# A fused retention and soft mixture-of-attention kernel: gates and scaling factors moved to the head of a step, logits copied with v, scaling split from transposing, three buffers of p, a new tail

## The chip, the cores and the metric

One core of one Trainium2 chip runs the whole program. The time is device microseconds of that core for one execution; lower is better. The engines are TensorE (PE, with weight loads PEld), VectorE (DVE), ScalarE (ACT), GpSimd (POOL), and SyncE (SP), whose queue issues every DMA. TensorE writes its results to PSUM, which has eight banks; a bank can be written again only when its readers are done.

## The reference

Inputs q, k, v have the shape [8, 8, 576, 64] (batch, heads, positions, width). Everything is float32.

```
ret  = (0.125 * q @ k.T) * gamma_h ** (i - j)   for i >= j, else 0
x    = (ret @ v), heads side by side            # [8, 576, 512]
g    = x @ w_gate                               # logits of 4 experts
w    = softmax over the two largest of g, 0 for the others
out  = sum over experts e of  w_e * softmax(causal(0.125 * (x wq_e)(x wk_e).T)) @ (x wv_e) @ wo_e
```

Each expert has a width of 64, so that two experts fill 128 partitions.

## The kernel before

**Chunks and steps.** A batch has five chunks of positions, t = 0 to 4: four of 128 and one of 64. The 40 chunks of the eight batches are numbered n = 5b + t. The main loop runs over steps n = 0 to 41; a step works on several chunks at once, each at another stage, so that all engines have something to do.

**What a step does, in the order in which it is written.** `load(n + 2)` brings q, k (tile x) and v, k (tile vk) of a later chunk. `qk(n)` makes the products of q and k of chunk n in blocks of 64 (L137), ScalarE copies them to p (L140), GpSimd masks them (L143). `result(n - 1)`, a generator called `late`, makes the retention output of the chunk before: products with the running state (`old`, L165, copied by ScalarE in L168), products with the masked p (`own`, L178), their sum on VectorE (L183), the scaling by gamma on GpSimd (L188), the split in two parts for a two-part multiplication (ScalarE L191, GpSimd L193), and on the way `decay` of a later chunk's v (GpSimd, L104). `state(n)` updates the running state (L117, VectorE L123 and L125). `scores(n - 6)` makes the attention scores of an older chunk m into PSUM (`ss`, L338, or L345 for t = 4), VectorE subtracts the row maximum on the way out of PSUM (L356, L360), ScalarE takes the exponential and its row sum (L364). `work(n)` holds the large matmuls: projections to q and k (`proj`, L235), the value projection (`vproj`, L260), the product of attention weights and values (`values`, L400) and the output projection (`outproj`, L420, copied out by ScalarE in L423). Its five steps are, by n mod 5: 3, projections of q and k for a batch's first two chunks; 0, value tiles of these (and half an output projection); 1, projections for the other three chunks; 2, value tiles of these, with `values` of the batch before woven in; 4, output projections.

**Gates and the scaling of p.** `vproj` makes the four logits beside the values in one PSUM bank; ScalarE copies the values to vn (L264), then VectorE copies the logits to lg (L265). After a group's last tile `gate` goes on a list. Each call of `gates()` advances every gate on the list by one phase: first seven VectorE operations (L292 to L301) and an exponential on ScalarE (L302), then nine small VectorE operations that end in the weights WT (L304 to L311). `spread(m)` of a chunk m first makes the factors, gate weight over row sum, in three small VectorE operations (L376 to L378). Then it goes through up to four blocks: scale the block of p32 (ScalarE, L385; for two blocks of t = 3 VectorE, L383) and transpose it in 32x32 pieces into TA or TB (VectorE, L387 and L389). `values` reads TA and TB. `spread` is a generator: `work` yields between groups of matmuls, and each yield lets it do one block. In a step with `values` the flag `hold` keeps all of `spread` until `work` is done, since the transposes overwrite what `values` still reads.

**Order.** PE, DVE, ACT and POOL execute their instructions in the order in which the Python code issues them (`manual_schedule`). SP's queue is ordered by the program's scheduler. PSUM tiles all come from one pool of eight banks.

**The end.** The last four chunks' scores and the last batch's products run in `tail(m)`, called for m = 36 to 40.

## Time and profile before

| | |
|---|---|
| median of three runs | 482.8 us (478.55, 484.5, 482.8) |
| the profiled execution | 481.82 us |
| its span in the trace | 478.3 us |
| busy: PE, PEld | 425.9 us (89%), 369.6 us (77%) |
| busy: DVE, ACT, POOL | 307.7 us (64%), 278.4 us (58%), 172.4 us (36%) |
| mean granted TensorE clock | 0.943 of full speed |
| moved by DMA | 66.73 MB, 140 GB/s over the span |

Busy times are unions of instructions; matmuls are pipelined, and PE counts as busy while one is under way, even where the next one is late. Time outside the span (481.82 less 478.3) is start and end of the program.

### The profile page before, as it was taken

What the parts mean: (1) busy time and instruction counts of PE and PEld (TensorE: products, weight loads), DVE (VectorE), ACT (ScalarE), POOL (GpSimd) and SP (SyncE); (2) the same over time, 40 slices, a digit from 0 to 9 for tenths busy, and PEclk for the clock granted to TensorE, in tenths of its full rate; (3) what the DMA queues carried; (4) which work ended last, traced back from release to release, by engine and by line L of the source; (5) the groups of instructions that cost most, each with busy time, mean ns of one, the idle gap of its engine ahead of it and who ended that gap; (6) DMA issues with size and microseconds to landing.
All of it is one profiled execution on the core that took longest, in us unless ns stands there. A gap on an engine that the chain in (4) does not pass through costs nothing. (4 is left out here: it accounts for less than half of the span.)

```text
span 478.3 us, 21378 instructions
## 1 busy us (share of the span) xinstructions
PE 425.9 (89%) x9068; PEld 369.6 (77%) x9068; DVE 307.7 (64%) x1219; ACT 278.4 (58%) x858; POOL 172.4 (36%) x198
## 2 busy tenths in 40 slices
PE   6687995998989988998989988998989989999566
PEld 3587984787879877987878877987879876986456
DVE  2743777954777476964776477963778477826750
ACT  1545666553866377653866377663766367726732
POOL 2428544541434334641444333551544432100000
PEclk9679997999989999999999999999989999899769
DMA  7926466332745264553544263641844041405211
GB/s 281 403 96 225 154 155 214 88 117 73 207 160 140 94 188 138 189 153 96 184 161 140 92 190 135 213 131 54 229 160 138 4 103 47 123 1 124 78 46 56
DMA packets 49246, 66.73 MB, mean 140 GB/s; under 512 B 4096, under 2 KB 38400, under 8 KB 49152
## 3 DMA queue, kind: packets, MB, share of 16 engines
q1 hardware_dynamic: 49152, 65.38, 43.0%
q8 instruction: 71, 1.16, 1.0%
q14 instruction: 23, 0.19, 0.1%
HBM read 50.68 MB, written 14.68 MB: 137 GB/s over the span
## 5 line engine op out<-in xcount | busy, mean ns | idle before, releaser
L364 ACT ACTIVATE p<-p,nm 128x64 f32<-128x64 f32 (+5 forms) x144 | 79.5, 553 | 76.9 <-DVE nm L356 56.2
L143 POOL TENSOR_SCALAR_AFFINE_SELECT p<-p 64x512 f32<-64x512 f32 (+1 forms) x80 | 48.8, 610 | 166.8 <-ACT p L140 164.2
L385 ACT ACTIVATE p<-p,sm 128x128 f32<-128x128 f32 (+7 forms) x128 | 63.4, 539 | 23.1 <-DVE sm L378 23.1
L387 DVE STREAM_TRANSPOSE ta<-p 128x256 f32<-128x256 f32 (+2 forms) x144 | 56.0, 394 | 28.9 <-ACT p L385 26.2
L183 DVE TENSOR_TENSOR x<-x,own 128x256 f32<-128x256 f32 (+1 forms) x80 | 26.4, 363 | 46.2 <-ACT x L168 40.2
L356 DVE CUSTOM_DVE_ANT_0 p<-ss,mask 128x128 f32<-128x128 f32 (+7 forms) x128 | 50.7, 452 | 4.0 <-PE ss L338 3.7
L188 POOL TENSOR_TENSOR x<-x,gi 128x512 f32<-128x512 f32 (+1 forms) x38 | 44.5, 1171 | 13.3 <-DVE x L183 10.0
L338 PE MATMUL ss<-k,q 64*64 64x64 f32 (+7 forms) x512 | 41.0, 408 | 4.5 <-ACT p L140 4.5
L178 PE MATMUL own<-p,vk 64*64 64x64 f32 x1152 | 31.8, 226 | 13.1 <-issue 5.6
L193 POOL TENSOR_TENSOR x1l<-x,x1h 128x512 fp32r<-128x512 f32 (+1 forms) x24 | 26.5, 1103 | 45.6 <-ACT x1h L191 45.6
L400 PE MATMUL ys<-ta,vq 32*64 32x288 f32 (+7 forms) x1152 | 35.4, 375 | 6.5 <-DVE ta L387 4.4
L178 PEld LDWEIGHTS own<-p,vk 64*64 64x64 f32 x1152 | 26.3, 137 | 15.7 <-issue 14.9
L264 ACT ACTIVATE vn<-pv 128x256 f32<-128x256 f32 x40 | 14.8, 371 | 39.5 <-PE pv L260 39.5
L400 PEld LDWEIGHTS ys<-ta,vq 32*64 32x64 f32 x1152 | 25.9, 149 | 12.8 <-issue 4.6
L117 PE MATMUL st<-vk 64*64 64x64 f32 x1024 | 27.0, 233 | 8.8 <-DVE vk L104 3.3
L265 DVE COPY lg<-pv 128x4 f32<-128x4 f32 x40 | 5.9, 149 | 43.9 <-ACT vn L264 43.4
L420 PE MATMUL po<-yh,who 128*128 128x320 f32 (+1 forms) x128 | 29.6, 312 | 3.5 <-ACT yh L408 3.5
L104 POOL TENSOR_TENSOR vk<-vk,con 128x512 f32<-128x512 f32 (+1 forms) x34 | 32.5, 956 | 0.1
L117 PEld LDWEIGHTS st<-vk 64*64 64x64 f32 x1024 | 23.1, 145 | 10.8 <-issue 4.2
L140 ACT ACTIVATE p<-qk 128x256 f32<-128x256 f32 (+1 forms) x80 | 24.3, 359 | 8.3 <-PE qk L137 8.3
L420 PEld LDWEIGHTS po<-yh,who 128*128 128x128 f32 x128 | 20.9, 194 | 10.4 <-issue 4.9
L423 ACT ACTIVATE ot<-po 128x256 f32<-128x256 f32 (+1 forms) x64 | 24.7, 403 | 7.1 <-PE po L420 5.7
(106 smaller groups left out, 1039.1 us busy)
## 6 DMA issues: line engine op xcount, KB each, us to landing
x<-xf SPq DMA_DIRECT2D x32, 512.0 KB, 4.4
vk<-vkf SPq DMA_DIRECT2D x32, 512.0 KB, 5.8
vq<-hv SPq DMA_DIRECT2D x32, 192.0 KB, 4.3
out<-ot SPq DMA_DIRECT2D x32, 160.0 KB, 2.2
vq<-hv SPq DMA_DIRECT2D x32, 128.0 KB, 3.4
out<-ot SPq DMA_DIRECT2D x32, 128.0 KB, 1.7
hv<-vn SPq DMA_DIRECT2D x8, 384.0 KB, 2.7
ta<-wraw SPq DMA_DIRECT2D x4, 512.0 KB, 8.2
```

Of the source, the lines that this page charges most:

```text
L104: (gp if n > 5 else v).tensor_mul(vv, vv, gam[:, 2 * c:2 * c + k].unsqueeze(3).to_broadcast([128, k, 4, D]))
L117: mm(ps[r][HALF[g], s, u], vk[HALF[r], s, 1, h], vk[HALF[r], s, 0, h], start=True, stop=True)
L143: gp.affine_select(w, w, pattern=[[0, 4 * k], [1, 64]], base=0, channel_multiplier=-1, compare_op=OP.is_ge, fill=0.0)
L178: mm(own[r][HALF[u], g, i], vk[HALF[r], s, 0, 2 * g + u], p[HALF[r], g, s, u], start=True, stop=True)
L188: e.tensor_mul(x32, x32, gi[:, :, t0:t0 + C])
L338: mm(ps[u][HALF[p]], q[p][HALF[z], l0 + 64 * i:l0 + 64 * i + 64], k[p][HALF[z], :ws[u]], start=True, stop=True)
L356: v.tensor_tensor_reduce(x, ps[u], mask[:, 512 - ws[u]:], -1.0, BIG, OP.add, OP.min, nm[:, u:u + 1])
L364: act(x, x, AF.Exp, bias=bias, scale=-1.0, accum_out=sm[:, 0, u:u + 1])
L385: act(x, x, AF.Copy, scale=rs[:, u:u + 1])
L387: v.transpose(TA[:, :min(nb, 8), z, k], x[:, :min(nb, 8)])
L400: mm(py[g][HALF[z], sj - s0:], vq[QUAD[g], jj, D * z:D * z + D], tt[QUAD[g]], start=(j == 0), stop=(j == 2 * s1 - 1))
L420: mm(ps, ww[:, p, d * 128:(d + 1) * 128], yy[:, p], start=(i == 0), stop=(i == 5))
```

## The change

`gates()` and the factors of the chunk that will be scaled in this step are called at the head of a step, ahead of `qk`, `result`, `state` and `scores`; a second call of `gates()` stands behind `scores`. A gate now has three phases: VectorE, the exponential alone, VectorE. ScalarE copies all 260 columns of the value bank; VectorE's copy of the logits is gone. `spread` is split in `factors`, `scale` and `turn`; in a step with `values`, `scale` runs beside `work` and only `turn` waits. p32 has three buffers in place of two, x and vk three in place of four. The projections of batch 1's first group, all in step 8 before, are shared by steps 8 and 9. The tail is one function with an order written out by hand.

```diff
-        X[n] = x = ld.tile([128, 2, 4, C], F32, name="x", tag="x", bufs=4)
+        X[n] = x = ld.tile([128, 2, 4, C], F32, name="x", tag="x", bufs=3)
-        VK[n] = vk = ld.tile([128, C // 64, 2, 4, D], F32, name="vk", tag="vk", bufs=4)
+        VK[n] = vk = ld.tile([128, C // 64, 2, 4, D], F32, name="vk", tag="vk", bufs=3)
...
-            VN[b, r] = (sb.tile([128, nt, E * D], F32, name=f"vn{r}", bufs=1),
-                        sb.tile([128, nt, E], F32, name="lg", tag="lg"),
+            VN[b, r] = (sb.tile([128, nt, NWV], F32, name=f"vn{r}", bufs=1),
                         sb.tile([128, 4 * nt, 2 * D], F32, name=f"vq{r}", bufs=2 - r))
-        vn, lg, vq = VN[b, r]
+        vn, vq = VN[b, r]
...
-        act(vn[:, ti], ps[:, :E * D], AF.Copy)
-        v.tensor_copy(lg[:, ti], ps[:, E * D:])
+        act(vn[:, ti], ps, AF.Copy)
...
-            nc.sync.dma_start(hv.rearrange("(t p) c -> p t c", p=128), vn)
+            nc.sync.dma_start(hv.rearrange("(t p) c -> p t c", p=128), vn[:, :, :E * D])
...
-        lg = VN[b, r][1]
+        lg = VN[b, r][0][:, :, E * D:]
...
+        yield False
         act(ex, ex, AF.Exp)
         yield False
...
-        p32 = sb.tile([128, n, w], F32, name="p32", tag="p32", bufs=2)
+        p32 = sb.tile([128, n, w], F32, name="p32", tag="p32", bufs=3)
...
-    def spread(m):
+    def factors(m):
         b, t = divmod(m, 5)
         r = 0 if t < 2 else 1
         ti = t - RNG[r][2][0]
-        p32, sm, ws = SS.pop(m)
+        p32, sm, ws = SS[m]
         n = len(ws)
         rs = sm[:, 1, :n]
         v.tensor_scalar(sm[:, 0, :n], sm[:, 0, :n], 1e-9, None, op0=OP.add)
         v.reciprocal(rs, sm[:, 0, :n])
         v.tensor_mul(rs, rs, WT[b, r][:, ti].rearrange("p i z -> p (i z)")[:, :n])
-        for u in range(n):
-            z, k, nb = u % 2, 2 * t + u // 2, ws[u] // 32
-            x = p32[:, u, :ws[u]]
-            if t == 3 and u < 2:
-                v.tensor_scalar(x, x, rs[:, u:u + 1], None, op0=OP.mult)
+
+    def scale(m):
+        p32, sm, ws = SS[m]
+        for u, w in enumerate(ws):
+            x = p32[:, u, :w]
+            if m % 5 == 3 and u < 2:
+                v.tensor_scalar(x, x, sm[:, 1, u:u + 1], None, op0=OP.mult)
             else:
-                act(x, x, AF.Copy, scale=rs[:, u:u + 1])
-            x = x.rearrange("p (j c) -> p j c", c=32)
+                act(x, x, AF.Copy, scale=sm[:, 1, u:u + 1])
+            yield
+
+    def turn(m):
+        p32, sm, ws = SS.pop(m)
+        for u, w in enumerate(ws):
+            z, k, nb = u % 2, 2 * (m % 5) + u // 2, w // 32
+            x = p32[:, u, :w].rearrange("p (j c) -> p j c", c=32)
             v.transpose(TA[:, :min(nb, 8), z, k], x[:, :min(nb, 8)])
             if nb > 8:
                 v.transpose(TB[:, :nb - 8, z, k - 4], x[:, 8:])
             yield
 
+    def spread(m):
+        a, b = scale(m), turn(m)
+        for _ in a:
+            next(b)
+            yield
+
...
-            if b or kind[-1] == "1" or kind in ("o0", "y"):
+            if n == 8:
+                STEPS[8], STEPS[9] = [(b, kind, 0)], [(b, kind, 1)]
+            elif b or kind[-1] == "1" or kind in ("o0", "y"):
                 STEPS.setdefault(n, []).append((b, kind, part))
...
-    def tail(m):
+    def tail():
         b = B - 1
-        if m < NC:
-            run(scores(m))
+        t0 = NC - 5
+
+        def beside(g, *hs):
+            for _ in g:
+                for h in hs:
+                    next(h, None)
+
+        def outs(b, r):
+            for d in range(4):
+                yield from outproj(b, r, d)
+
         gates()
-        hold = m == NC - 4
-        spreads = spread(m - 1)
-        for n in {NC - 4: (NC + 2,), NC - 3: (NC + 4,), NC - 2: (NC + 5,)}.get(m, ()):
-            for _ in work(n):
-                if not hold:
-                    next(spreads, None)
-        if m == NC - 1:
-            run(values(b, 0, 4))
-            for d in range(4):
-                run(outproj(b, 0, d))
-        run(spreads)
-        if m == NC:
-            run(values(b, 4, 9))
-            for d in range(4):
-                run(outproj(b, 1, d))
+        factors(t0)
+        run(scores(t0 + 1))
+        sc = scale(t0)
+        ys = values(b - 1, 0, 9)
+        for t in RNG[1][2]:
+            beside(vproj(b, 1, t), sc)
+            next(ys, None)
+            if t == 3:
+                run(scores(t0 + 2))
+        factors(t0 + 1)
+        gates()
+        run(scale(t0 + 1))
+        gates()
+        run(turn(t0))
+        run(turn(t0 + 1))
+        gates()
+        factors(t0 + 2)
+        run(scores(t0 + 3))
+        beside(outs(b - 1, 0), spread(t0 + 2))
+        run(scores(t0 + 4))
+        factors(t0 + 3)
+        beside(outs(b - 1, 1), spread(t0 + 3))
+        run(values(b, 0, 4))
+        factors(t0 + 4)
+        beside(outs(b, 0), spread(t0 + 4))
+        run(values(b, 4, 9))
+        run(outs(b, 1))
 
...
         late = result(n - 1) if 1 <= n <= NC else iter(())
+        gates()
+        if n > LAG:
+            factors(n - LAG - 1)
...
         if n >= LAG:
             run(scores(n - LAG))
+        gates()
         if n > 5:
             run(late)
         else:
             decay(n + 1)
-        gates()
         for w in {2: "kq", 3: "v", 6: "o"}.get(n, ""):
             weights(w, "l" if w == "k" else "hl")
-        spreads = spread(n - LAG - 1) if n > LAG else iter(())
-        hold = any(kind == "y" for _, kind, _ in STEPS.get(n, []))
+        spreads, turns = iter(()), iter(())
+        if n > LAG:
+            if any(kind == "y" for _, kind, _ in STEPS.get(n, [])):
+                spreads, turns = scale(n - LAG - 1), turn(n - LAG - 1)
+            else:
+                spreads = spread(n - LAG - 1)
         for _ in work(n):
-            if not hold:
-                next(spreads, None)
+            next(spreads, None)
         run(spreads)
+        run(turns)
         run(late)
-    for m in range(NC - 4, NC + 1):
-        tail(m)
+    tail()
 
 
 def _layout(inputs):
```

## Rows read from the trace of the kernel before

**Rows 1.** Windows: start:end, length, busy us (instructions) by engine, granted clock, DMA

```profile
250.00:300.00 50.00, 45.84 (x1079) 40.20 (x1081) 32.59 (x135) 30.41 (x98) 19.98 (x23) 0.97 0.44 139
82.20:85.70 3.50, 3.50 (x21) 2.56 (x22) 2.73 (x13) 0.63 (x4) 3.04 (x4) 0.51 0.01 2
461.10:468.00 6.90, 4.46 (x128) 4.17 (x136) 2.43 (x9) 1.44 (x2) 0.00 (x0) 0.51 0.01 2
```

**Rows 2.** Waits, all of the span: who waited for whom, us in total, times, longest

```profile
ACT p L385 <- DVE sm L378: 23.1, 24, 1.8
...
PE own L178 <- ACT ot L423: 3.2, 6, 0.7
...
PE own L178 <- DVE lg L265: 1.8, 2, 1.0
```

**Rows 3.** Timeline, 274 to 285 us, after values: start, length, instruction [idle before <-releaser]

```profile
275.44 1.55 DVE L409 TENSOR_TENSOR yl<-ys,yh 128x288 fp32r<-128x288 f32 x4 [1.05 <-ACT yh L408]
...
277.50 1.17 ACT L385 ACTIVATE p<-p,sm 128x64 f32<-128x64 f32 x4 [1.19 <-DVE sm L378]
277.88 1.14 DVE L387 STREAM_TRANSPOSE ta<-p 128x64 f32<-128x64 f32 x4 [0.41 <-ACT p L385]
...
278.99 1.68 PE L338 MATMUL ss<-k,q 64*64 64x320 f32 x16 [1.27 <-ACT p L140]
...
279.84 0.75 DVE L183 TENSOR_TENSOR x<-x,own 128x256 f32<-128x256 f32 x2 [0.82 <-ACT x L168]
...
280.61 0.74 PE L235 MATMUL pj<-xh,whk 128*128 128x256 f32 x4
...
283.08 0.20 DVE L292 TENSOR_TENSOR gd<-lg 128x48 f32<-128x48 f32 x1
...
284.54 0.16 DVE L378 TENSOR_TENSOR sm<-sm,wt 128x4 f32<-128x4 f32 x1
```

**Rows 4.** Timeline, 286 to 295 us: chunk of t = 3 beside output projections

```profile
288.43 0.75 DVE L183 TENSOR_TENSOR x<-x,own 128x256 f32<-128x256 f32 x2 [1.28 <-ACT x L168]
...
291.41 0.27 DVE L304 SCALAR_TENSOR_TENSOR ex<-rk,ex 128x12 f32<-128x12 f32 x1
...
293.25 1.28 POOL L193 TENSOR_TENSOR x1l<-x,x1h 128x512 fp32r<-128x512 f32 x1 [1.60 <-ACT x1h L191]
...
293.44 1.11 DVE L378 TENSOR_TENSOR sm<-sm,wt 128x4 f32<-128x4 f32 x1
...
294.58 0.56 ACT L385 ACTIVATE p<-p,sm 128x320 f32<-128x320 f32 x1 [1.15 <-DVE sm L378]
```

**Rows 5.** Groups by form, VectorE: busy us, mean ns of one, idle before

```profile
L301 DVE TENSOR_TENSOR ex<-lg,mx 128x8 f32<-128x8 f32 x8 | 7.5, 940 | 0.3
```

**Rows 6.** Timeline, 79 to 85 us: step 9 into step 10

```profile
79.83 2.02 ACT L385 ACTIVATE p<-p,sm 128x320 f32<-128x320 f32 x4 [1.39 <-DVE sm L378]
...
82.17 2.46 PE L345 MATMUL ss<-k,q 64*64 64x288 f32 x16 [4.52 <-ACT p L140]
```

**Rows 7.** Timeline of the tail, 432 to 465 us

```profile
432.74 1.41 PE L338 MATMUL ss<-k,q 64*64 64x320 f32 x16
...
433.24 1.55 DVE L409 TENSOR_TENSOR yl<-ys,yh 128x288 fp32r<-128x288 f32 x4 [1.05 <-ACT yh L408]
...
443.44 0.62 DVE L356 CUSTOM_DVE_ANT_0 p<-ss,mask 128x448 f32<-128x448 f32 x1
...
445.76 0.17 DVE L304 SCALAR_TENSOR_TENSOR ex<-rk,ex 128x12 f32<-128x12 f32 x1
...
447.27 0.17 DVE L376 TENSOR_SCALAR sm<-sm 128x4 f32<-128x4 f32 x1
...
460.18 0.45 DVE L387 STREAM_TRANSPOSE ta<-p 128x256 f32<-128x256 f32 x1 [2.17 <-ACT p L385]
...
463.54 4.72 PE L400 MATMUL ys<-ta,vq 32*64 32x160 f32 x124 [4.42 <-DVE ta L387]
```

**Rows 8.** The page, DMA issues: KB each, median us from issue to landing

```profile
vk<-vkf SPq DMA_DIRECT2D x32, 512.0 KB, 5.8
```

More of the change, by code (lines that the diff above doesn't have):

```diff
@@ L395, in values @@
             sj = max(s0, j // 2)
-            vq, jj = VN[b, 0 if j < 8 else 1][2], j % 8 if j < 8 else j - 8
+            vq, jj = VN[b, 0 if j < 8 else 1][1], j % 8 if j < 8 else j - 8
             for z in range(2):
```

## The prediction

> **What bounds the kernel now.** I read the windows first, for the middle of the run and for stretches at a low clock, then the list of waits, then the timeline of the places where that list puts the waits of TensorE. In the middle, PE is busy 45.84 of 50 us at a granted clock of 0.97, while DVE has 32.59 and ACT 30.41 [rows 1]. So there are about 4 us in 50 that PE does not fill, and an edit on another engine can win only out of these, out of stretches at half clock, and out of the two ends. The waits that name the lines of the change are: ACT's scaling behind the factors, 23.1 us in 24 places; PE's own product behind the copy of the logits, 1.8 us in two, and behind ACT's copies of output projections, 3.2 us in six [rows 2]. The large one is a wait of ACT, which is not the bound; what it is worth has to be read in the places where PE waits for ACT afterwards. There are two such places in each batch, and then the ramp and the tail.
>
> **After values (the step with n mod 5 = 3), six times in the main loop.** Before, VectorE finishes yl at 276.99, then makes the factors, ACT scales four blocks (1.17 us), VectorE transposes them, and only behind the scalings does ACT copy the new qk banks; the scores wait 1.27 us for that bank and start at 278.99 [rows 3]. The change takes scaling away from here: it runs beside the value tiles, on an ACT that waits there anyway. The scores could then start some 1.3 us earlier. But the next projection (280.61) starts only when the scores are through and VectorE's L183, at 279.84, has freed own's bank, and L183 has a new line in front of it: four transposes (1.14 us) and, at the head of the step, the first phase of the gate with the factors, which here took from 283.08 to 284.70, 1.62 us [rows 3]. 276.99 + 1.14 + 1.62 = 279.75 against 279.84. With the overlap of adjoining VectorE operations I take 0.15 us a batch, **0.9 us** in all. The ends are 0 (L183 is no earlier) and 1.27 x 6 = 7.6 us (the projection gets another bank); the value lies near the first, because the line in front of L183 adds up to what stood there.
>
> **The chunk of t = 3 beside output projections (n mod 5 = 4), six times.** Here VectorE does the row maxima, then the last gate phase and the factors, from 291.41 to 294.55, 3.14 us; ACT meanwhile stands 1.15 us before its first scaling at 294.58, and behind the scalings come the copies of six output banks for which PE waits in the next step [rows 2, 4]. One of these factor operations, L378, took 1.11 us against 0.16 us elsewhere, exactly while GpSimd ran L193 from 293.25 for 1.28 us [rows 3, 4]; L301 in its narrower form has a mean of 940 ns over eight [rows 5]. Moved to the head of the step these operations have no such neighbour in this timeline, so the line is 3.14 - 0.95 = 2.19 us. VectorE sat idle 1.28 us before L183 there [rows 4]; the rest, 0.91 us, delays L183, the maxima and the exponentials. ACT, free at 293.43 before (294.58 - 1.15), is then free at 294.34 and need not wait: 0.24 us earlier than 294.58. Six times that is **1.5 us**. The ends: the whole wait of 1.15 us, 6.9 us in all, and a loss of 0.91 us each, 5.5 us, if PE has to wait for the bank that L183 frees. I take the sum along the line, since both its halves come from this very step.
>
> The Trainium skill, in SBUF — State Buffer, section Who interferes with whom, says that a VectorE instruction with two inputs from SBUF contends with a GpSimd instruction that reads SBUF, and that the one issued first blocks the other for its whole length. The trace agrees for L378 beside L193. The same rule speaks against the new place if GpSimd's masking of p falls beside it; by it the moved line would keep its 3.14 us, ACT would be free 1.86 us later at 295.29, and these steps would lose 0.7 us each, 4.3 in all, instead of winning 1.5.
>
> **Logits copied with v.** A value bank is now free when ACT has copied it, not when VectorE comes to L265 behind its transposes. The two waits of PE on that copy go: **1.8 us** [rows 2]; the ends are 0, where another reader of the bank is as late, and 1.8, as no other wait of that list's kind is on PE's own product. Four more columns for ACT on 256 are under 2% of a copy that PE is not waiting for. The DMA to HBM still takes rows of 256 values.
>
> **The ramp.** Step 9 had no projections; ACT waited 1.39 us for the factors, and PE stood idle 4.52 us before the scores at 82.17 [rows 6], then ran at a granted clock of 0.51 until 85.7 [rows 1]. Two projections now fill part of that gap. ACT's chain, which ends the gap, gains the same 0.24 us as above. Whether the clock stays up is not shown; that is worth half of 3.5 us, 1.75. I take both, **2.0 us**, since more than half of the gap is filled; the ends are 0.5 us lost (the projections' copies stand in ACT's queue) and 4.5 us, all of the gap.
>
> **Buffers.** A third p32 lets a scaled but not yet transposed chunk wait; without it the next exponentials would have to. For x and vk one buffer less means that a load starts when `own` of the chunk before is through, one step nearer to its use. A vk load lands 5.8 us after its issue [rows 8], and a step is 8.6 us from one L183 to the next (279.84 to 288.43) [rows 3, 4], with the first use behind L183 of the following step. So SP's queue holds the load at its head, and nothing behind it is wanted before it goes. Nothing, with 1 us lost in the filling as the other end; if that cover goes, it is 5.8 us less what remains of the step.
>
> **The tail.** Chunk 37's scores (1.41 us) go ahead of the last value tile, so yl ends at about 434.79 + 1.41 = 436.2 [rows 7]. Then VectorE does, in the new order: factors and first phase (1.62) [rows 3], transposes of chunk 35 (1.14) [rows 3] and of chunk 36 (estimate 1.7, from the same row and three times the columns at a part-fixed cost), the last phase (445.76 to 447.27, 1.5 us) [rows 7], factors (0.5). That is 6.5 us, so chunk 38's maxima start at 442.7 against 443.44. From there to the last values it took 20.1 us (463.54) [rows 7]; this held the last gate phase, 1.5 us, now ahead, and 2.17 us in which VectorE waited at 460.18 for scalings that stood behind four output copies, where copies and scalings now alternate [rows 7]. Of these 3.7 us I give back 1.1, the wait for the copy yh that stays (1.05 there) [rows 7]. 0.75 + 2.6 = 3.3 us. The last values ran at a clock of 0.51 with PE busy 4.46 us [rows 1]; a wait shorter than 4.42 us may leave part of that at full speed, up to 2.2 us, of which I take 0.7. Together **4.0 us**. The ends are 6.7 us (3.7 + 0.75 + 2.2) and 2.2 us lost, if the wait for chunk 38's maxima makes another such stretch.
>
> That wait exists: PE has made four output projections by about 440 and needs a bank for chunk 39's scores, which the maxima from 442.7 on set free. The Trainium skill, in TensorE: Matmul & The Clock Gate, Part 1, says that the throttled state is the default and activity releases it; by that the tail would win 1.1 us instead of 4.0. The trace agrees that half clock follows an idle PE, at 82.2 [rows 1, 6].
>
> **Sum.** 0.9 + 1.5 + 1.8 + 2.0 + 4.0 = 10.2 us. The profiled execution took 481.8 us, 1.0 under the median of 482.8; 481.8 - 10.2 = **471.6 us**, 2.3% under the median. About 2%, that is below 473.1 or above 492.5, can be told from no change here.
>
> **The rivals.** *Only a moved wait, 0.24.* VectorE's line at the head takes all that ACT gains; both places in the batch and the ramp give nothing, and 1.8 + 4.0 stay: 476.0 us. For it: L183 comes out at the same time above. Against it: L378 loses its neighbour.
>
> *More than the line, 0.15.* ACT's whole wait of 1.15 us goes in the t = 3 steps (6.9), and the tail has its upper end (6.7): with 0.9, 1.8 and 2.0 that is 18.3 us, 463.5 us. For it: idle VectorE at other heads. Against: the 0.91 us that L183 is late.
>
> *The tail gives nothing of weight, 0.05.* Another half-clock stretch of the size seen, 2.2 us, and none of the 0.7: 4.0 - 2.9 = 1.1 us, so 474.5 us.
>
> *Slower, 0.06.* PE waits for the banks that VectorE frees late, in the t = 3 step and in one more with a gate phase, 0.91 us each, and falls to half clock once a batch, 1.75 us: 3.6 us six times, 21.4 us, less 1.8 + 2.0 + 4.0: 495 us. It decides from 3.1 us a batch on. Against it: PE is at the long projections when these banks are wanted.
>
> That the change does not do what it says could hold for the split of scaling alone: if ACT reached those scalings only after the value tiles, the first place would stay as it is. It changes the sum by 0.9 and has no chance of its own.
>
> **Chances.** The forecast has 0.50, with a range of its own from 467 to 476; about seven tenths of it lie under 473.1. With the case above it and a small part of the others, faster gets 0.54, within 2% 0.40, slower 0.06. The range from 462 to 480 takes in the moved wait, the tail's case and the larger gain, and leaves out the slower case and the outer ends.
>
> **What would show it.** After values, scores that follow the state products at once and a projection that starts with L183's end: right; a projection at the scores' end: I gave too little. In the t = 3 step, L378 at 0.16 us and a scaling without a wait on the factors; if PE's waits on output copies stay, only the 0.24 us came. In the ramp, a clock that stays up in step 10. In the tail, the last values at about 460. A PE that waits on L183 or on the maxima in the middle of the run, or loads that land after their use, would prove the sum wrong.

## The result, and the profile after

The changed kernel takes 467.12 us (median of four runs, 465.14 to 467.85) beside 483.65 us for the kernel before (four runs, 478.55 to 485.94): a ratio of 0.9686, 95% interval 0.9601 to 0.9771, faster. The forecast was 471.6 us, its range 462 to 480. The profiled execution took 466.81 us, its span is 464.9 us, its mean granted clock 0.960 (before 481.82, 478.3 and 0.943). Of the 15.0 us between the two, 13.4 lie in the span; outside it stood 3.5 us before and 1.9 after, and since later runs of the kernel before have 1.7 to 3.0 us there, I don't ascribe the 1.6 to the change. Of all the runs reported here one, of a later kernel at 470.96 us, counts as slow and is left out of that kernel's median.

I cut both spans at the first qk product (L137) of a step:

| stretch | before | after | gain | forecast |
|---|---|---|---|---|
| start to step 8 | 61.09 | 59.99 | 1.1 | 0 |
| step 8 to 12 (ramp) | 38.12 | 35.15 | 3.0 | 2.0 |
| step 12 to 39 | 295.43 | 289.64 | 5.8 | 0.9 + 1.5 + 1.8 = 4.2 |
| step 39 to the end | 83.69 | 80.14 | 3.6 | 4.0 |

In the kernels run below step 8 starts from 2.3 us earlier to 0.9 us later than before, up to 2.7 us apart with the same first steps; whether the first line is an effect stays open. In the middle a step with n mod 5 = 3 went from 11.57 to 10.91 us (five of six), one with 4 from 7.78 to 7.88; where no half-clock stretch falls into it, one with 0 went from 10.34 to 10.03, and the one with 1 behind it from 10.02 to 9.75 (n = 26: from 11.02, with a wait of 1.04 us on the copy of the logits, to 9.75). From 75 us on, stretches at half clock (granted 0.50, 1.2 of 2.4 GHz) add up to 37.7 us before and 23.9 after; at 1.2 of 2.4 GHz each costs at most half its length, so up to 6.9 of the 13.4 us came that way, through whichever step.

The windows of the changed kernel, with the columns of [rows 1]: the middle, a stretch of the tail, and the last values.

```profile
242.70:292.70 50.00, 46.35 (x1088) 40.25 (x1087) 30.09 (x134) 30.08 (x98) 20.30 (x24) 1.00 0.47 142
...
445.80:452.60 6.80, 6.71 (x48) 6.11 (x56) 3.35 (x13) 3.23 (x9) 0.00 (x0) 0.50 0.32 113
...
451.90:458.00 6.10, 5.56 (x291) 5.06 (x290) 0.66 (x3) 1.28 (x5) 0.00 (x0) 0.94 0.15 48
```

PE fills half a us more of 50 than in [rows 1], VectorE works 2.5 us less, and the last values run at 0.94, not 0.51; the half clock has moved ahead of them, to the projections behind a wait of 2 us. Its waits:

```profile
ACT p L386 <- DVE sm L377: 1.3, 1, 1.3
...
PE pj L235 <- DVE x L183: 2.8, 4, 1.0
...
PE own L178 <- ACT ot L436: 2.8, 6, 0.5
```

ScalarE's 23.1 us behind the factors [rows 2] are gone. The wait on output copies stays (3.2 before), the one on the copy of logits is not listed any more, and TensorE now waits for L183 before the projection, which it did not before (only the weight loads did, 3.6 us in six places; now 6.7). The timeline shows it, after values and in the step with t = 3:

```profile
320.84 1.55 DVE L422 TENSOR_TENSOR yl<-ys,yh 128x288 fp32r<-128x288 f32 x4 [9.34 <-ACT yh L421]
...
322.31 0.75 DVE L394 STREAM_TRANSPOSE ta<-p 128x64 f32<-128x64 f32 x4
...
322.98 0.17 DVE L290 TENSOR_TENSOR gd<-vn 128x48 f32<-128x48 f32 x1
...
323.52 1.34 PE L337 MATMUL ss<-k,q 64*64 64x320 f32 x13
...
324.78 0.16 DVE L377 TENSOR_TENSOR sm<-sm,wt 128x4 f32<-128x4 f32 x1
324.89 0.75 DVE L183 TENSOR_TENSOR x<-x,own 128x256 f32<-128x256 f32 x2
325.36 0.73 PE L235 MATMUL pj<-xh,whk 128*128 128x256 f32 x4 [0.50 <-DVE x L183]
...
334.20 0.17 DVE L377 TENSOR_TENSOR sm<-sm,wt 128x4 f32<-128x4 f32 x1
334.31 0.75 DVE L183 TENSOR_TENSOR x<-x,own 128x256 f32<-128x256 f32 x2
...
339.15 0.55 ACT L386 ACTIVATE p<-p,sm 128x320 f32<-128x320 f32 x1
```

From the start of yl to the first projection it is 4.52 us; in [rows 3] 280.61 - 275.44 = 5.17. The scores follow the state products without a wait, and the projection starts 0.47 us into L183, which stands behind gate phase and factors (322.98 to 324.94). In the step with t = 3 the last factor takes 0.17 us where it took 1.11 [rows 4], and the scaling waits for nothing. The ramp and the last values:

```profile
72.06 0.16 DVE L377 TENSOR_TENSOR sm<-sm,wt 128x4 f32<-128x4 f32 x1
...
76.75 1.00 ACT L386 ACTIVATE p<-p,sm 128x320 f32<-128x320 f32 x2
...
79.88 1.54 PE L344 MATMUL ss<-k,q 64*64 64x288 f32 x15
...
451.91 2.79 PE L413 MATMUL ys<-ta,vq 32*64 32x160 f32 x128
454.48 2.55 PE L413 MATMUL ys<-tb,vq 32*64 32x160 f32 x160
```

In the ramp the factors are made at 72 us and ScalarE scales at 76.75, where it began at 79.83 [rows 6]. The last values start 451.91 - 384.78 = 67.1 us behind step 39, before 463.54 - 394.64 = 68.9 [rows 7].

### The profile page after: what moved, and what is told of

It is laid out like the page before. It is cut to its first block, busy times and chain, and to the rows that moved or that the text cites. A ratio compares the mean times of both kernels' runs of the same rounds, so it can differ in the third digit from the quotient of the medians.

```text
span 464.9 us, 21312 instructions
## 1 busy us (share of the span) xinstructions
PE 422.9 (91%) x9068; PEld 365.9 (79%) x9068; DVE 279.8 (60%) x1179; ACT 275.7 (59%) x858; POOL 173.5 (37%) x198
## 5 line engine op out<-in xcount | busy, mean ns | idle before, releaser
L394 DVE STREAM_TRANSPOSE ta<-p 128x256 f32<-128x256 f32 (+2 forms) x144 | 53.4, 388 | 59.0 <-ACT p L386 56.5
L422 DVE TENSOR_TENSOR yl<-ys,yh 128x288 fp32r<-128x288 f32 (+2 forms) x36 | 12.7, 414 | 63.9 <-ACT yh L421 63.9
L337 PE MATMUL ss<-k,q 64*64 64x512 f32 (+7 forms) x512 | 41.8, 409 | 3.0 <-issue 1.1
L178 PE MATMUL own<-p,vk 64*64 64x64 f32 x1152 | 30.5, 222 | 8.4 <-issue 4.6
L183 DVE TENSOR_TENSOR x<-x,own 128x256 f32<-128x256 f32 (+1 forms) x80 | 26.2, 361 | 19.6 <-ACT x L168 19.6
L263 ACT ACTIVATE vn<-pv 128x260 f32<-128x260 f32 x40 | 14.9, 374 | 29.0 <-PE pv L259 28.9
L413 PE MATMUL ys<-ta,vq 32*64 32x288 f32 (+8 forms) x1152 | 31.3, 349 | 0.2 <-DVE nm L359 0.2
L436 ACT ACTIVATE ot<-po 128x256 f32<-128x256 f32 (+1 forms) x64 | 24.5, 400 | 8.7 <-PE po L433 5.5
L433 PE MATMUL po<-yl,who 128*128 128x320 f32 (+1 forms) x128 | 29.2, 310 | 0.0
```

The costliest lines, as they stand in the source:

```text
L178: mm(own[r][HALF[u], g, i], vk[HALF[r], s, 0, 2 * g + u], p[HALF[r], g, s, u], start=True, stop=True)
L337: mm(ps[u][HALF[p]], q[p][HALF[z], l0 + 64 * i:l0 + 64 * i + 64], k[p][HALF[z], :ws[u]], start=True, stop=True)
L394: v.transpose(TA[:, :min(nb, 8), z, k], x[:, :min(nb, 8)])
L413: mm(py[g][HALF[z], sj - s0:], vq[QUAD[g], jj, D * z:D * z + D], tt[QUAD[g]], start=(j == 0), stop=(j == 2 * s1 - 1))
L433: mm(ps, ww[:, p, d * 128:(d + 1) * 128], yy[:, p], start=(i == 0), stop=(i == 5))
```

## The experiments

**My theory** after this reading: the middle is won after values, where ScalarE's scalings no longer wait for factors behind yl; the ramp and the tail are won apart from it. **The rivals**: the new places at the head carry it; the split carries it; or what looks like a gain is only where half-clock stretches fell. "Step 3" below is a step with n mod 5 = 3; L183, yl and the projection are as above. Times are medians of four runs (VectorE copies logits: three), ratios to the kernel before on the same chip (480.0 to 480.8 us) with their interval. The changed kernel was not run again beside them (its kernel before had 483.65 us), so a difference of some 3 us between one of these times and its 467.1 shows nothing by itself; step lengths can be compared.

| kernel | us | ratio | step 3 (n = 23, 28) | yl to projection |
|---|---|---|---|---|
| before | 480.0 to 480.8 | | 11.57, 11.57 | 5.17 |
| factors alone | 475.49 | 0.989 (0.984 to 0.995) | 10.25, 10.26 | 3.87 |
| tail alone | 474.45 | 0.987 (0.980 to 0.994) | 11.57, 11.57 | |
| both | 470.04 | 0.978 (0.971 to 0.984) | 10.24, 10.25 | |
| changed, old tail | 470.61 | 0.978 (0.973 to 0.984) | 10.91, 10.91 | |
| changed, old places | 467.53 | 0.973 (0.967 to 0.978) | 9.80, 9.92 | 3.53 |
| changed, scaling kept back | 464.21 | 0.965 (0.959 to 0.970) | 10.74, 10.73 | 4.34 |
| changed, sum first | 475.31 | 0.987 (0.980 to 0.994) | 9.79, 10.18 | |
| changed, VectorE copies logits | 466.35 | 0.970 (0.963 to 0.978) | 10.91, 10.92 | |
| changed, step 8 undivided | 465.43 | 0.967 (0.961 to 0.973) | 10.91, 10.90 | |
| new places in the ramp only | 465.13 | 0.967 (0.964 to 0.970) | 9.80, 9.79 | |

The table has n = 23 and 28, where the gain is largest. In n = 13, 18 and 38 most of these kernels have a wait of TensorE without a releaser, or scores held up in their course, and gain less: with the factors alone these steps take 10.82, 10.97 and 11.24 us (11.56 or 11.57 before); n = 33 waits for VectorE there, before too. The last section says what these waits are.

**The factors alone**, in the kernel before: in the steps with values, ahead of the value tiles.

```diff
+        if hold:
+            factors(n - LAG - 1)
-        spreads = spread(n - LAG - 1) if n > LAG else iter(())
+        spreads = spread(n - LAG - 1, hold) if n > LAG else iter(())
```

> The kernel before with one edit: in the steps with values (n mod 5 = 2) the three factor operations of VectorE are issued ahead of the value tiles and not behind yl; nothing else moves (scaling and transposes stay behind the values). Theory: before, ScalarE's four scalings waited for these three operations, which stood behind yl in VectorE's line, and its copies of the next qk and old banks stood behind the scalings; so this alone shortens the next step (n mod 5 = 3) from 11.57 to between 10.25 and 10.9 us, as in the runs with old places and with kept-back scaling: six times 0.7 to 1.3 us, 4 to 8 us less than before on the same chip, 473 to 477 us beside 480 to 481. Rival (the three buffers of p32 did it in the run with the new tail): that step stays at 11.5 us and the time at 480 us.

```profile
272.55 1.55 DVE L417 TENSOR_TENSOR yl<-ys,yh 128x288 fp32r<-128x288 f32 x4 [1.05 <-ACT yh L416]
...
273.29 1.18 ACT L393 ACTIVATE p<-p,sm 128x64 f32<-128x64 f32 x4
...
274.80 1.69 PE L338 MATMUL ss<-k,q 64*64 64x320 f32 x16
...
276.42 0.73 PE L235 MATMUL pj<-xh,whk 128*128 128x256 f32 x4
```

This is the timeline after values. The scalings start 0.74 us behind yl's start, before 277.50 - 275.44 = 2.06 [rows 3]; scores and projection come as much earlier, 1.3 us. Three small operations moved, 5.2 us won (4.0 of them in the profile up to step 39): the theory stands, and the split is not needed for it. The 1.3 us are those of n = 23 and 28; in n = 13, 18 and 38 it is 0.7, 0.6 and 0.3 us.

**The tail alone**, in the kernel before, and **both**:

```diff
-        X[n] = x = ld.tile([128, 2, 4, C], F32, name="x", tag="x", bufs=4)
+        X[n] = x = ld.tile([128, 2, 4, C], F32, name="x", tag="x", bufs=3)
...
-        p32 = sb.tile([128, n, w], F32, name="p32", tag="p32", bufs=2)
+        p32 = sb.tile([128, n, w], F32, name="p32", tag="p32", bufs=3)
...
-    for m in range(NC - 4, NC + 1):
-        tail(m)
+    tail()
```

> The kernel before with the new tail and its buffers (three of p32, x and vk) again, but the factors of the main loop behind yl, as in the kernel before. Theory (the factors ahead of the value tiles gave the middle its part in the run with the new tail): the steps with n mod 5 = 3 take 11.5 us, step 39 starts as before within 0.6 us save for half-clock stretches, and only the end is shorter, by 2 to 3.5 us: 477 to 478.5 us beside a before of 480 to 481. Rival (the buffers gave the middle its part): 10.2 to 11 us in these steps and 470 us in all.

> The kernel before with the new tail alone, and the buffers that it needs (three of p32, three of x and vk); gates, factors, scaling, logits and steps 8 and 9 as before. Theory (the tail and the buffers are independent of the rest): up to step 39 as before within 0.5 us, so three buffers of x and vk cost nothing, and from step 39 to the end of the span 80 to 81 us in place of 83.7: 3 us less than before, 477 to 478 us beside a before of 480 to 481 on the same chip. Rival (the tail's gain hangs on the new gate phases or on the logits): 480 us or more. Rival (fewer buffers of x and vk cost something in the filling that the other parts covered): steps 3 to 12 come 1 us or more later than before.

In the run called "both" I had put the factors of the main loop ahead of `work`, which its expectation doesn't say; so it missed by 7 us, and this led to the two single runs. With the tail alone step 3 stays at 11.57 us in all six, and step 39 starts 0.1 us later than before: the buffers cost nothing and give nothing. All of its 5.5 us of span lie behind step 39, more than expected; there its stretches at half clock add up to 13.7 us, in the kernel before to 20.6, so up to 3.5 of the 5.5 us can be the clock's doing.

**The old tail** in the changed kernel (one more call of `gates()` at m = 37):

```diff
-    tail()
+    for m in range(NC - 4, NC + 1):
+        tail(m)
```

> The changed kernel with the old tail (one more call of the gates in it, since a gate has three phases now). Theory: up to step 39 nothing differs from the changed kernel (its qk product starts near 384.8 us), and from there to the end of the span it takes about 3.5 us more again, as in the kernel before (83.7 against 80.1 us): span about 468.5, time 470 to 471 us. Rival (the tail's saving was a half-clock stretch that fell otherwise): 467 to 468 us.

The time came as expected, 470.61 us, span 468.6, but not from where I expected it. Step 39 starts at 387.82, 3.0 us later than in the changed kernel, whose code is the same up to there (2.0 of the 3.0 before step 8), and from step 39 to the end it is 80.8 us, only 0.6 more. So this hit is luck, and the run does not show what the tail is worth. The wait of [rows 7] for the last transposes is back in the list of waits:

```profile
PE ys L413 <- DVE ta L394: 4.5, 1, 4.5
```

**The old places** in the changed kernel:

```diff
-        gates()
-        if n > LAG:
-            factors(n - LAG - 1)
...
+        gates()
         for w in {2: "kq", 3: "v", 6: "o"}.get(n, ""):
...
         if n > LAG:
+            factors(n - LAG - 1)
```

> The changed kernel with the gate phases and the factors at their old places (one call behind scores and late, two phases, factors ahead of work); the split of scaling and transposing, the buffers, the step 8/9 split and the new tail stay. Theory (VectorE's line bounds the step after values, and the split of scaling shortened it): without the 1.6 us of gate phase and factors in front, L183 comes right behind the transposes, the projection is then bound by the end of the scores, and the step with n mod 5 = 3 keeps its shorter length or loses another 0.3 us: 10.6 to 10.95 us against 10.93 after and 11.57 before. In the steps with n mod 5 = 4 ScalarE waits for the factors again (about 1 us each). Time 465 to 469 us. Rival (the new places carry the gain): that step goes back to about 11.5 us and the time to 470.5 to 472 us.

The first theory held for the time, and by more than the 0.3 us expected in two of the six steps (9.80 and 9.92 us); the four others take 10.46 to 11.27. Timeline after values, and in the ramp:

```profile
270.64 1.55 DVE L421 TENSOR_TENSOR yl<-ys,yh 128x288 fp32r<-128x288 f32 x4 [6.22 <-ACT yh L420]
...
272.78 0.75 DVE L183 TENSOR_TENSOR x<-x,own 128x256 f32<-128x256 f32 x2
...
274.17 0.74 PE L235 MATMUL pj<-xh,whk 128*128 128x256 f32 x4
...
79.40 1.01 ACT L385 ACTIVATE p<-p,sm 128x320 f32<-128x320 f32 x2 [2.16 <-DVE sm L376]
...
82.92 2.13 PE L343 MATMUL ss<-k,q 64*64 64x288 f32 x14
```

L183 starts 2.14 us behind yl's start, in the changed kernel 4.05: gate phase and factors at the head cost the projection 1.0 us here. In the steps with t = 3, ScalarE waits for the factors again (24.5 us in 21 places of the span) and yet these steps take 7.82 us, not more than the 7.88 of the changed kernel. What the head is good for is the ramp: with the old places the scores start at 82.92, though step 9 has the two projections; step 8 to 12 takes 37.4 us against 35.2. So the two effects cancel, 467.5 against 467.1 us.

**Scaling kept back** (`turns = spread(...)` in steps with values, nothing beside the value tiles):

```diff
-                spreads, turns = scale(n - LAG - 1), turn(n - LAG - 1)
+                turns = spread(n - LAG - 1)
```

> The changed kernel with scaling kept behind the value tiles again, together with the transposes, in the steps with values; the factors stay at the head of the step. Theory: ScalarE's four scalings stand ahead of its copies of the qk banks again, the scores start 0.4 to 0.8 us later, their end and not L183 bounds the projection, and the step with n mod 5 = 3 takes 11.1 to 11.35 us against 10.93 after and 11.57 before; the rest of the old length was the factors ahead of the scalings. Six times 0.2 to 0.4: time 468 to 470 us. Rival (the split is the whole of that place): 11.5 us or more, time 471 us. Rival (scaling is hidden either way): 10.9 us and 467 us.

```profile
267.45 1.55 DVE L422 TENSOR_TENSOR yl<-ys,yh 128x288 fp32r<-128x288 f32 x4 [9.57 <-ACT yh L421]
...
271.33 0.74 DVE L183 TENSOR_TENSOR x<-x,own 128x256 f32<-128x256 f32 x2
271.79 0.38 PE L235 MATMUL pj<-xh,whk 128*128 128x256 f32 x1 [0.41 <-DVE x L183]
```

The last expectation came nearest, and the step is even 0.18 us shorter than with the split, since L183, behind the head, sets the projection in both and comes 3.88 us behind yl's start rather than 4.05. Beside the head the split is worth nothing. Up to step 39 the run is 1.7 us ahead of the changed kernel. The other 3.6 us of its profile lie in the tail, whose code is the same, with 6.8 us at half clock in place of 13.7: that much of a single run can be the clock's doing.

**The sum first**: head behind L183 in the steps with n mod 5 = 3.

```diff
+        first = n % 5 != 3 or n <= LAG
+        if first:
+            head()
...
             next(late, None)
+            if not first:
+                head()
```

> The changed kernel with the head's gate phase and factors put behind the sum L183 in the steps with n mod 5 = 3, ahead of the state; all else stays. Theory (VectorE's line in front of L183 is what the projection waits for now): L183 starts 1.6 us earlier there, the projection starts with the end of the scores, about 0.35 to 0.5 us earlier, the waits of the projections on L183 go; the maxima and exponentials are no later. Six times that is 2 to 3 us: 464 to 465 us. Rival (another reader of the bank, or ScalarE's later start, takes its place): no change, 467 us. Rival on the other side: VectorE's state sums, now behind the gate phase, come late for the next value tiles or the scores: 468 us.

It wins its step and loses more in the next (9.67 and 9.60 us for n = 24 and 29, where the changed kernel has 7.88; 8.12 and 8.49 for n = 14 and 19): the time is 8 us longer than the changed kernel's. The timeline, in the step that starts at 272.10 and in the next:

```profile
276.39 0.74 PE L235 MATMUL pj<-xh,whk 128*128 128x256 f32 x4
...
279.09 0.48 DVE L355 CUSTOM_DVE_ANT_0 p<-ss,mask 128x320 f32<-128x320 f32 x1
...
283.75 0.33 PE L178 MATMUL own<-p,vk 64*64 64x64 f32 x4 [0.55 <-ACT k L240]
...
284.82 0.62 PE L178 MATMUL own<-p,vk 64*64 64x64 f32 x26 [0.73 <-ACT q L242]
```

The maxima start 7.0 us behind the first qk product; in the changed kernel 6.0 (326.35 - 320.34). The exponentials, and ScalarE's copies of the projections behind them, are late by as much, and PE waits for the banks. A third course, that I had priced at 1 us.

**VectorE copies the logits** again, and **step 8 undivided**, each in the changed kernel:

```diff
-        act(vn[:, ti], ps, AF.Copy)
+        act(vn[:, ti, :E * D], ps[:, :E * D], AF.Copy)
+        v.tensor_copy(vn[:, ti, E * D:], ps[:, E * D:])
```

> The changed kernel with the logits copied by VectorE again (256 columns by ScalarE, four by VectorE, into the same tile). Theory: this copy stands in VectorE's line behind transposes and holds a value bank; the gain of the change in the steps with n mod 5 = 0 (10.34 us before, 10.03 to 10.05 after, where no half-clock stretch falls into them) is its removal, since that step's length stayed at 10.02 when the gates went back to their old places: so 10.3 us again, 1.8 us in six, time 468.5 to 469 us. Rival (the bank is wanted later than either copy): 10.05 us, time 467 us, and the 0.3 us come from elsewhere.

```diff
-            if n == 8:
-                STEPS[8], STEPS[9] = [(b, kind, 0)], [(b, kind, 1)]
-            elif b or kind[-1] == "1" or kind in ("o0", "y"):
+            if b or kind[-1] == "1" or kind in ("o0", "y"):
```

> The changed kernel with both of batch 1's first projections in step 8 again. Theory: TensorE's gap ahead of step 10's scores comes back; the stretch from the qk product of step 8 to that of step 12 takes about 2 to 3 us more than after (35.2 us after, 38.1 before), half of it a longer stretch at half clock; time 469 to 470 us. Rival (the gap is bound by ScalarE's chain and not by work for TensorE): 35.2 us and 467 us.

With the copy on VectorE the steps with n mod 5 = 0 keep their length (10.04 us for n = 25): there the rival held. But in step 26, where the kernel before waited 1.04 us for this copy, a wait on it is in the list, under the tile that it writes here:

```profile
PE own L178 <- DVE vn L264: 0.5, 1, 0.5
```

That step takes 10.18 us, in the changed kernel 9.75, so the copy is worth 0.4 us in one place. For step 8 the rival held. With step 8 undivided the stretch from 8 to 12 takes 35.3 us, and the time is no longer than that of the changed kernel. Here the scores start at 79.83, 19.1 us behind step 8, in the changed kernel 19.9:

```profile
77.50 2.01 ACT L386 ACTIVATE p<-p,sm 128x320 f32<-128x320 f32 x4
79.42 0.63 ACT L140 ACTIVATE p<-qk 128x256 f32<-128x256 f32 x2
79.83 2.46 PE L344 MATMUL ss<-k,q 64*64 64x288 f32 x16 [2.62 <-ACT p L140]
```

**New places in the ramp only**, the version that the runs point to: head up to step 12, old places from 13 on.

```diff
+        early = n < 13
+        if early:
+            gates()
+            if n > LAG:
+                factors(n - LAG - 1)
...
+        if not early:
+            gates()
+            gates()
```

> The changed kernel with the new places of gates and factors up to step 12 alone, and the old places (behind scores and late, both first phases together; factors ahead of work) from step 13 on; split, logits, buffers, step 8/9 and tail as changed. Theory, from the runs with old places throughout: where the scaling is split off, the gate phase and factors at the head only lengthen VectorE's line in front of L183, some 0.8 us a batch, while in the ramp the head is worth 2.5 us (8 to 12). So the ramp of the changed kernel (step 12's start near 95.1 us) and steps with n mod 5 = 3 of 9.8 to 10.5 us in place of 10.9: five batches at 0.6 to 0.8, 463 to 464.5 us. Rival (TensorE only shifts a wait into the next steps, or the shorter steps draw more half-clock stretches): 466 to 468 us.

Step 12 starts at 95.09 and steps 23 and 28 take 9.8 us; up to step 39 it is 2.7 us ahead of the changed kernel. The time of 465.13 us is 2.0 under the changed kernel's, and the intervals overlap. One line of its waits tells of the logits: in step 11 PE waits for ScalarE's copy of the values, as it had for VectorE's of the logits (1.0 us). It costs nothing there: steps 10 and 11 together take 20.46 us, in the changed kernel, without this wait, 20.47.

```profile
PE st L117 <- ACT vn L263: 1.1, 1, 1.1
```

**Matmuls in the tail's gaps**, on top of that version, to hold the clock:

```diff
+    def fill(n):
+        for i in range(n):
+            mm(LAST[0][:, :256], wz, wz[:, None, :].to_broadcast([128, 2, 128]), start=True, stop=True)
...
+        fill(18)
         run(scores(t0 + 4))
...
+        fill(12)
         factors(t0 + 4)
```

> The kernel with new places up to step 12 alone, and 30 matmuls of zero weights (256 columns each) that write an output bank already copied out: 18 in TensorE's wait of 3.25 us for the maxima ahead of chunk 39's scores, 12 in its wait of 2.2 us for yh ahead of the last output projections but four. They compute nothing that is read. Theory (an idle TensorE draws the half-clock stretches of the tail): the stretches that began at 432.5 and 442.7 us without the fillers are gone or shorter, and the last 35 us take 1.5 to 4 us less: 461.5 to 463.5 us in place of 465.1. Rival (the stretch comes whatever stands in the gap, or the fillers overrun it): 465 to 467 us, with the same two stretches.

```profile
436.37 4.00 PE L429 MATMUL po<-wz 128*128 128x256 bf16 x18 [8.48 <-ACT ot L442]
...
447.14 1.49 PE L429 MATMUL po<-wz 128*128 128x256 bf16 x12
```

Slower, 470.4 us (0.978, 0.971 to 0.984), by a fault of mine: the first 18 waited for an output copy that stands behind exponentials in ScalarE's queue, and held up the scores. So this run does not judge the theory there. Behind the 12, the projections ran at full clock, 448.38 to 451.4 us.

**Maxima first in the tail**, with ten such matmuls at the second place only:

```diff
         run(turn(t0))
+        run(scores(t0 + 3))
         run(turn(t0 + 1))
         gates()
         factors(t0 + 2)
-        run(scores(t0 + 3))
```

> The kernel with new places up to step 12 alone and two edits in the tail: chunk 38's maxima and exponentials stand ahead of chunk 36's transposes, the last gate phase and the factors; and ten zero-weight matmuls of 256 columns, which compute nothing that is read, stand ahead of the last output projections but four (the 18 others of the run with fillers are left out, since they waited 8.5 us for an output copy and held up the scores). Theory (in the tail TensorE waits for the maxima behind VectorE's line, and the idle stretch draws a low clock): the maxima start about 2.8 us earlier, near 427.4 where it was 430.3, TensorE's wait ahead of chunk 39's scores shrinks from 3.1 to under 1 us, and the output projections behind the ten matmuls run at full clock (3 us in place of 6): 3 to 5 us less than 465.1, 460 to 462 us. Rival (the chain through the last gate phase, the factors and the scalings of chunk 37 sets the end, and it is now 2.4 us later on VectorE): 465 to 466 us.

```profile
428.27 2.48 PE L344 MATMUL ss<-k,q 64*64 64x288 f32 x16 [0.17 <-DVE nm L355]
...
434.14 0.89 PE L439 MATMUL po<-yh,who 128*128 128x320 f32 x2 [1.54 <-ACT ot L442]
...
446.59 2.79 PE L413 MATMUL ys<-ta,vq 32*64 32x160 f32 x124
...
451.40 1.80 PE L413 MATMUL ys<-tb,vq 32*64 32x160 f32 x128 [1.34 <-issue]
...
454.87 0.24 PE L413 MATMUL ys<-tb,vq 32*64 32x32 f32 x2 [1.67 <-issue]
```

Most of it came as the theory had it: the wait for the maxima is 0.17 us, no half clock falls between 437.6 and 461.5, the last values start at 446.59, where the version that it builds on had 449.35 (1.1 us of that is there at step 39 already); against it, a wait of 1.54 us for an output copy is new, with two smaller ones 3.3 us in all. And the time is the same, 465.65 us (0.971, 0.968 to 0.973; five runs). The gain was given back in the last values: PE waited twice, 3.0 us together, with no releaser in the list, and their last product comes at 454.87. So the time is that of my rival and the cause is not: a third bound, of which the last section tells.

## Why the prediction was right, and where not

The sign and the size of the whole were right; the terms came out differently. That the sum fell into the range is in part luck: two terms, of 1.5 and 1.8 us, gave little or nothing, others gave more than forecast, and up to 6.9 us between the two profiles can be half clock that fell elsewhere.

**After values: the mechanism was half seen, the term too small.** Forecast 0.15 us a batch, measured 0.65 in five of six steps. The step that failed is the comparison of L183 with L183 (279.75 against 279.84). Before, the projection did not wait for L183 but for the end of the scores (278.99 + 1.68 = 280.67), and those for ScalarE, whose four scalings had waited 1.19 us for the factors, a row that I quoted [rows 3]. I counted the factors in VectorE's line only, not as what ScalarE's queue was waiting for. Alone they are worth up to 1.3 us a step; the head then takes part of it back, which I had right in kind: the line of VectorE in front of L183 is the new bound.

**The step with t = 3: the rows came true, the gain did not come from them.** The last factor operation lost its neighbour and took 0.17 us, with GpSimd idle beside it (333.75 to 335.23); by that the trace agrees with the Trainium skill (SBUF — State Buffer, Who interferes with whom). Last gate phase and factors took 2.30 us (332.06 to 334.36; I had 2.19), ScalarE waits no longer; and the step became 0.1 us longer. The next became 0.3 us shorter, but it is as short (10.02) with the gates at their old places. Which part of the change brings those 0.3 us stays open: no kernel that takes one part away loses them. The time lies between the forecast and the rival "more than the line" (463.5 us), but that rival's mechanism, ScalarE's whole wait won in these steps, did not come about.

**Logits: 0.4 us in place of 1.8.** The two waits of PE [rows 2] stand in step 8 (0.79 us) and in step 26 (1.04). The first names the copy only as the last to come: with the old places it is there with the copy on ScalarE too (0.58 us), and with the copy back on VectorE in the changed kernel it is gone. Of the second, 0.50 us come back with the copy, and 0.4 us of the step's length; the rest of the 1.3 us that this step won goes with a VectorE that is earlier there: it made the copy 2.10 us behind the first qk product before, 1.26 in that run.

**Ramp: 3.0 us, but not by the projections.** I took 1.75 us for a clock that stays up and 0.24 for ScalarE's chain. The clock did not stay up (3.4 us at half clock from 80.6 us on), and it matters little: with the scaling kept back no such stretch falls into the ramp, and it takes 35.2 us as well. Undividing step 8 costs nothing, the old places cost 2.3 us. The gap ends with ScalarE's chain, and the factors ahead of the maxima shorten it: with the old places ScalarE waits 2.16 us for them there.

**Buffers: nothing, as forecast. Tail: 3.6 us in place of 4.0** between the two profiles, of which half is shown. From step 39 to the last values it is 1.8 us less (I had 3.3), from there to the end 1.8 us less, at full clock in place of half (I had 0.7). The second holds throughout: 14.1 to 15.2 us in the three kernels with the old tail, 13.0 to 13.7 in the nine with the new one and nothing filled in. The first does not: the old tail needs 65.6 to 70.9 us to the last values and the new one 63.5 to 68.4, and the changed kernel with the old tail is there 1.5 us sooner than with the new. How much of that half is the tail's doing stays open. The wait for chunk 38's maxima that I named is there, 3.1 us in the changed kernel. By the rule of the Trainium skill that I weighed (TensorE: Matmul & The Clock Gate, Part 1) the tail would have won 1.1 us; it came out better, and the rule itself is not contradicted: behind the wait of 2 us that is left a stretch at 0.50 follows, behind the same wait filled with matmuls none.

**Slower** did not come about, but the sum put first shows that its mechanism exists: late banks in the step with t = 3 cost 1.6 to 1.8 us in three of the batches.

## What to carry to other kernels

When an in-order engine waits for a small operation of another, price the operation by what is queued behind the waiting engine, not by its own length: three operations of 0.5 us together held up to 1.3 us of TensorE's time in a batch. Moving work to the head of a step helps where the engine idles there (the ramp) and costs where a late result stands behind it; try each move alone, since here two that look like one change cancelled. Take a wait's named releaser as the last to come, and measure how much of the wait is its own: of 1.04 us behind the copy of the logits it was 0.4. And where a run's time comes as expected, look whether it came at the expected place: that of the old tail did not.

## What the runs showed of the hardware that I had not expected

TensorE can be held up with no releaser in the list of waits: 3.0 us in the last values, 288 products with weights of 32x64 that take 5.1 us in the changed kernel. The two kernels with matmuls filled into the tail lost 3.0 and 2.4 us there, the version without them 0.20 us.

The trace ties these waits to instructions. The profile's page lists a DMA queue of that kind, here for the changed kernel with its packets and MB:

```profile
q8 instruction: 71, 1.16, 1.1%
```

By the trace's packet times such packets, of 16 KB, landed in the last values of the kernel with maxima first at 449.91 and 453.44, and TensorE went on at 451.40 and 454.87, 1.49 and 1.43 us later. In the fourteen profiles TensorE waited 65 times for more than 0.6 us without a releaser; 57 of these waits ended 1.2 to 1.7 us behind the landing of such a packet, and the other eight all stand in step 10. The same is what kept the gain small in steps 13, 18 and 38: with the factors alone a packet landed at 168.34, in the course of step 18's scores, and their next weight load came at 169.84. Why it is these packets and not others that are late is not shown.

The Trainium skill, in Runtime: NRT & Kernel Launch, section Instruction fetch mechanics, says that an engine fetches its own instructions while it runs and that the cost of this is mostly hidden. The trace agrees for most packets: in the changed kernel five of the 71 are followed by such a wait. It disagrees for the last values of the two filled kernels, where two packets in a row cost 3.0 and 2.4 us.

A stretch at half clock moves from run to run: four runs of one kernel (the sum put first) spread over 7 us, 470.59 us at a mean granted clock of 0.967 and 474.58 to 477.37 at 0.945 to 0.946, and the same tail took 76.5 or 80.1 us, with 6.8 or 13.7 us at half clock.
